# Attention into channel mix: whole-head value products in 64x64 tiles, natural channel order, and a new order of all tasks

## The chip, the cores and the metric

The kernel runs on one core of a Trainium2 chip. The metric is the device time of one execution in microseconds. Of the core's engines, PE multiplies matrices into PSUM, DVE, ACT and POOL work on vectors (POOL cannot read PSUM), and SP issues the DMAs. PEld is PE's loading of stationary operands.

## What is computed

Eight batches, eight heads, 576 positions, 64 channels a head. Causal attention in blocks of 64 positions feeds a channel mix over 512 channels:

```python
scores = scale * np.matmul(q, k.transpose(0, 1, 3, 2))
mask = block_i >= block_j                 # blocks of 64 positions
attn = np.exp(scores - max)               # masked
attn = attn / (np.sum(attn, axis=-1, keepdims=True) + 1e-09)
x = np.matmul(attn, v)                    # heads side by side: (B, S, 512)

xk = mu_k * x + (1.0 - mu_k) * x_prev     # x_prev: x one position earlier
xr = mu_r * x + (1.0 - mu_r) * x_prev
k = np.maximum(xk @ w_k, 0.0)             # 512 -> 1024
v = k * k @ w_v                           # 1024 -> 512
r = 1.0 / (1.0 + np.exp(-(xr @ w_r)))
out = r * v
```

## The kernel before, in words

The program is a list of some 930 tasks, each tied to an engine. Two tables drive it. ORDER is the sequence in which the tasks are issued, and so the order in which each engine's queue holds them; an entry `n+f` puts f filler products (128x512, of the identity matrix, read by nobody, L260) ahead of task n on PE. PLACE names the engine of each task that may run on several (A for ACT, D for DVE, P for POOL). Each engine works through its queue strictly in order; a task waits for its inputs and for its buffers. Buffers come in rings: "ld" (6 landing tiles for loads), "nl" (4 casts of q and k), "e" (exponentials, 16), "s" (3 PSUM tiles of two banks), "mm" (2 PSUM tiles of one bank), "xt", "d", "kr", "t", "o" and so on. A slot is free again when the last task that uses it has run.

Per batch b, the attention half goes as follows.

- Loads and turns: q and k are loaded and cast to bf16 (L247 on ACT, L251 on DVE and POOL), turned by PE against the identity (L354, into an "s" tile), and copied out (L247, L251) into "qkt". For batches 5 to 7 a DMA turns them instead. v is cast into "vo".
- Scores and exponentials: 12 units per batch. PE multiplies 64x64 tiles, four at a time (L413, an "s" tile); ACT takes the exponential of up to 1024 columns (L422) into an "e" tile.
- Sums, task "av S": with the constant `pick` PE sums the exponentials of each query over keys (L467, 128x32 tiles, 76 instructions), in three stretches of 192 positions; then it does the first 64 positions' products with the values. The rest of those products are tasks "av A" and "av B" (L478). A tile is 64x32: the 64 channels of a head are split into the even ones and the odd ones, f = 0 and 1, and A is f = 0 for all heads, B is f = 1. Each of S, A and B takes one "s" tile.
- Normalization on DVE: transpose the sums (t1, L507), take reciprocals (L512), transpose them back while they are spread over 32 rows (t2, L524), then three norms: T for the first 64 positions out of S (L536), A and B for the rest (L546), into "xt".
- Mix: the difference of neighbouring positions, one for each f (L568, POOL or DVE), and eight DVE pieces that write XK and XR (L585), one for each of four channel groups and of the two mixes.

The channel half works in nine chunks c of 512 positions: eight products with w_k ("pk", L632), relu (ACT L610 or DVE L612), squares (ACT L618, POOL or DVE L620), four products with w_r ("pr", L654) and a tanh (L663), four with w_v ("pv", L682), and the output on DVE (L690) and its store. A chunk's pk needs all four channel groups of XK for its positions, so chunk 0 starts when batch 0 is normalized and mixed, and chunk 1 needs batch 1. PE's queue interleaves the channel half of earlier positions with the attention half of later batches.

## Time and profile before

| what | value |
|---|---|
| median of 3 runs (range) | 264.22 us (263.5 to 264.7) |
| the profiled execution | 264.32 us, of which the span 262.5 us |
| busy in the span: PE, DVE, ACT, POOL | 246.8, 182.9, 180.4, 88.9 us |
| exponentials (L422) on ACT | 87.9 us |
| products with values (L478), instructions | 1280 |
| fillers (L260), instructions | 32 |

A busy time is the union of an engine's instructions. Matmuls are pipelined: several are in flight at once, so the mean time of one says little of their cost, which is read from how long a row of them takes. A row "a <-b" names in front what an instruction writes and behind what it reads; "[... <-X]" at its end is idle time of its engine and what ended it. The chain of waits is followed back from the last instruction: each row of it names a start, a length and the work that the end then hung on.

### The profile page before, as it was taken

How to read it: one execution, taken by the hardware profiler on the slowest of the kernel's cores; microseconds unless marked ns; L12 is line 12 of the kernel's file. 1: busy time of each engine (PE TensorE's matmuls, PEld its weight loads, DVE VectorE, ACT ScalarE, POOL GpSimd, SP SyncE). 2: the span in 40 equal slices, each digit the busy share in tenths (PEclk: the TensorE clock that was granted, in tenths of full speed). 3: DMA queues.
4: the chain of work that ended last, by engine and by line, in shares of the span. 5: the costliest groups of instructions: out<-in, count | busy, mean ns of one | idle time of the engine just before them, and what ended most of it. 6: DMA issues, size and time to landing. Idle time of an engine off the chain costs nothing.

```text
span 262.5 us, 7947 instructions
## 1 busy us (share of the span) xinstructions
PE 246.8 (94%) x3468; PEld 125.7 (48%) x3468; DVE 182.9 (70%) x245; ACT 180.4 (69%) x236; POOL 88.9 (34%) x71
## 2 busy tenths in 40 slices
PE   7687875999999999999999999999999999999995
PEld 2444643554545644544454446545544464444443
DVE  0153699589783897779889777496978497964423
ACT  1889897679888797857579897887457950460630
POOL 1115067169418600361531124802620246210130
PEclk9899999899999999999999999999999999999999
DMA  7999899799569993991999889976919200203105
GB/s 262 382 281 286 186 266 283 271 283 211 175 149 256 194 277 83 248 189 51 223 257 225 107 175 233 216 168 112 238 48 227 114 5 2 80 0 145 55 16 190
DMA packets 93428, 47.06 MB, mean 179 GB/s; under 512 B 81232, under 2 KB 81488, under 8 KB 93392
## 3 DMA queue, kind: packets, MB, share of 16 engines
q1 hardware_dynamic: 93392, 46.54, 73.0%
q8 instruction: 27, 0.44, 0.8%
q14 instruction: 9, 0.07, 0.1%
HBM read 33.56 MB, written 9.44 MB: 164 GB/s over the span
## 4 chain that ended last, share of the span: by engine, by line
PE 77%; DVE 7%; POOL 6%; ACT 5%; issue 2%; DMA 2%; SPq 0%; POOLq 0%; DVEq 0%
PE t_mm L632 23%; PE t_mm L682 21%; PE t_mm L654 11%; PE t_s L478 7%; PE t_s L413 7%; PE t_s L467 4%; ACT t_e L422 3%; PE t_s L354 3%; DVE XK L585 3%; DMA t_ld<-in_k_dram 2%; POOL t_k L620 2%; POOL t_d L568 2%; POOL t_nl L251 2%; ACT t_nl L247 1%; DVE t_o L690 1%
## 5 line engine op out<-in xcount | busy, mean ns | idle before, releaser
L422 ACT ACTIVATE t_e<-t_s 128x1024 f16<-128x1024 f32 (+1 forms) x96 | 87.9, 974 | 15.9 <-PE t_s L413 15.6
L632 PE MATMUL t_mm<-XK,WK 128*128 128x512 f16 x288 | 68.9, 383 | 1.8 <-POOL WK L251 1.2
L620 POOL TENSOR_TENSOR t_k<-t_kr 128x512 f16<-128x512 f32 x34 | 38.5, 1140 | 87.9 <-ACT t_kr L610 50.3
L682 PE MATMUL t_mm<-WV,t_k 128*128 128x512 f16 (+1 forms) x296 | 65.8, 374 | 0.3 <-POOL t_k L620 0.3
L610 ACT ACTIVATE t_kr<-t_mm 128x512 f32<-128x512 f32 x55 | 32.9, 598 | 27.3 <-PE t_mm L632 25.7
L632 PEld LDWEIGHTS <-WK 128*128 128x128 f16 x288 | 26.9, 98 | 36.1 <-issue 6.9
L682 PEld LDWEIGHTS <-t_k 128*128 128x128 f16 x296 | 28.0, 98 | 33.1 <-issue 1.9
L690 DVE SCALAR_TENSOR_TENSOR t_o<-t_t,t_mm 128x512 f32<-128x512 f32 (+1 forms) x37 | 24.6, 670 | 19.0 <-PE t_mm L682 13.7
L251 POOL CAST t_nl<-t_ld 128x1152 bf16<-128x1152 f32 x14 | 18.3, 1313 | 51.0 <-DVE XK L585 16.1
L663 ACT ACTIVATE t_t<-t_mm 128x512 f32<-128x512 f32 x36 | 21.5, 599 | 20.3 <-PE t_mm L654 20.0
L654 PE MATMUL t_mm<-WR,XR 128*128 128x512 f16 x144 | 34.9, 380 | 0.0
L585 DVE SCALAR_TENSOR_TENSOR XK<-t_d,MU,t_xt 128x576 f16<-128x576 f32 (+2 forms) x40 | 32.2, 834 | 1.5 <-POOL t_d L568 1.4
L413 PE MATMUL t_s<-t_qkt 64*64 64x64 bf16 (+7 forms) x640 | 29.2, 290 | 2.9 <-ACT t_e L422 1.8
L585 DVE SCALAR_TENSOR_TENSOR XR<-t_d,MU,t_xt 128x576 f16<-128x576 f32 (+2 forms) x40 | 29.5, 749 | 2.9 <-POOL t_d L568 2.9
L568 POOL TENSOR_TENSOR t_d<-t_xt 128x1152 f32<-128x1152 f32 x10 | 22.9, 2298 | 14.5 <-DVE t_xt L546 9.2
L413 PEld LDWEIGHTS <-t_qkt 64*64 64x64 bf16 x640 | 14.7, 106 | 20.2 <-issue 16.2
L478 PE MATMUL t_s<-t_e,t_vo 64*32 64x64 f16 (+7 forms) x1280 | 23.0, 284 | 0.0
L546 DVE TENSOR_TENSOR t_xt<-t_s,t_rt 128x1024 f32<-128x1024 f32 x16 | 19.4, 1220 | 5.0 <-PE t_s L478 4.6
L478 PEld LDWEIGHTS <-t_vo 64*32 64x32 f16 x1280 | 17.1, 92 | 7.2 <-issue 2.5
L654 PEld LDWEIGHTS <-XR 128*128 128x128 f16 x144 | 13.0, 98 | 15.4 <-issue 1.5
L354 PE MATMUL t_s<-identb,t_nl 128*128 128x128 bf16 x180 | 14.5, 237 | 5.5 <-ACT t_nl L247 2.4
L620 DVE TENSOR_TENSOR t_k<-t_kr 128x512 f16<-128x512 f32 x19 | 15.5, 832 | 6.1 <-ACT t_kr L610 5.8
(35 smaller groups left out, 177.9 us busy)
## 6 DMA issues: line engine op xcount, KB each, us to landing
t_ld<-in_v_dram SPq DMA_DIRECT2D x32, 288.0 KB, 5.9
out_dram<-t_o SPq DMA_DIRECT2D x35, 256.0 KB, 2.5
t_ld<-in_q_dram SPq DMA_DIRECT2D x10, 576.0 KB, 6.6
t_ld<-in_k_dram SPq DMA_DIRECT2D x10, 576.0 KB, 6.5
t_ld<-in_q_dram SPq DMA_DIRECT2D x12, 288.0 KB, 4.9
t_ld<-in_k_dram SPq DMA_DIRECT2D x12, 288.0 KB, 5.0
t_ld<-in_moe_w_k_dram SPq DMA_DIRECT2D x4, 512.0 KB, 6.9
t_ld<-in_moe_w_v_dram SPq DMA_DIRECT2D x4, 512.0 KB, 4.8
```

Source lines behind the costliest of these rows:

```text
L251: return e.tensor_copy(dst, src)
L413: nc.tensor.matmul(PS[g * D:g * D + D, x, col:col + n], qkt[rows, ka:ka + D], qkt[rows, qa:qa + n], start=True, stop=True)
L422: nc.scalar.activation(new(ebuf[key])[:, :, 0:width], new(m)[:, :, 0:width], AF.Exp, scale=ISQ)
L478: nc.tensor.matmul(dst(slice(c * QC, (c + 1) * QC), u, f, q0, n), weights(b, u, c, t, f), new(ebuf[key])[u * D:u * D + D, x, col:col + n], ...
L568: return e.tensor_tensor(new(d)[:, 0:2 * n].rearrange("p (u t) -> p u t", u=2), x[:, :, 1 + lo:1 + hi], x[:, :, lo:hi], ALU.subtract)
L585: return nc.vector.scalar_tensor_tensor((XK, XR)[kr][:, cc, g:g + w], new(d)[:, u * n + at - lo:u * n + at - lo + w], MU1[:, kr, cc:cc + 1 ...
L610: nc.scalar.activation(new(kr), new(m), AF.Relu)
L620: return e.tensor_tensor(dst(), KR, KR, ALU.mult)
L632: nc.tensor.matmul(ps, WK[:, cc, jc * P:(jc + 1) * P], XK[:, cc, at:at + CH], start=(cc == 0), stop=(cc == CCn - 1))
L654: nc.tensor.matmul(ps, XR[:, cc, g % R:g % R + P], WR[:, cc], start=(cc == 0), stop=(cc == CCn - 1))
L682: nc.tensor.matmul(ps[:, 0:w], k2[:, jc, jt * P:(jt + 1) * P], WV[:, jc, cols], start=(jc == 0), stop=(jc == JCn - 1))
L690: nc.vector.scalar_tensor_tensor(new(o)[:, 0:w], new(tb)[:, cols], 1.0, new(m)[:, 0:w], ALU.add, ALU.mult)
```

## The change

The products with values no longer split a head into even and odd channels. A tile is 64x64, a whole head; task A is now the even heads of each pair (x = 0), B the odd ones (x = 1), each for all rows of S and of its own tile. With that the channels stand in natural order, and the weights are loaded as two runs of 128 rows instead of 128 pairs of rows. The sums go in two stretches of 288 positions (60 instructions). Because two heads now lie on 64 rows each, the reciprocals are needed in two spreads, one for each x: after the reciprocal come a copy and four copies of 32 rows, then two transposes ("t2" for x = 0 and 1), each followed by a norm in two parts, first the tail out of S and then the rest. Both norms read S. mu_k and mu_r are loaded as rows and turned by one small product on PE. The ring "e" shrinks from 16 to 14, "rt" grows from 1 to 2. ORDER and PLACE are new throughout; there are 50 fillers.

```diff
-RINGS = {"ld": 6, "nl": 4, "qkt": 2, "vo": 2, "e": 16, "xt": 2, "tt": 1,
-         "rc": 2, "rt": 1, "d": 2, "kr": 5, "k2": 1, "t": 4, "o": 4,
+RINGS = {"ld": 6, "nl": 4, "qkt": 2, "vo": 2, "e": 14, "xt": 2, "tt": 1,
+         "rc": 2, "rt": 2, "d": 2, "kr": 5, "k2": 1, "t": 4, "o": 4,
 ORDER = """
-30 2 6 7 3 4+14 10 11 12 5 13 14 15 97 98 16 17 8 9 64+4 65 62 63 56 57
+3 4 5+14 6 7 8 11 12 13+9 14 15 9 10 16 17 18 45+5 46 53 49 50 47+2 48
...
-    QW = S // 3
+    NS = 2
+    QW = S // NS
...
     def mus(eng, me):
         for n, src in enumerate((moe_mu_k, moe_mu_r)):
-            nc.sync.dma_start(
-                MU[:, n].rearrange("p (g f) -> p g f", f=2),
-                src.rearrange("(g p f) -> p g f", g=2, f=2))
+            nc.sync.dma_start(MUR[CCn * n:CCn * n + CCn, :],
+                              src.rearrange("(c p) -> c p", p=P))
+    mu_rows = add("mus", "SP", mus)
+    mu_ps = plan.buf("mm")
+
+    def mut(eng, me):
+
+        nc.tensor.matmul(new(mu_ps)[:, 0:2 * CCn], MUR[:, :], identf,
+                         is_transpose=True, start=True, stop=True)
...
-                "(g p f) j -> g p f j", g=2, f=2)
+                "(g f p) j -> g p f j", g=2, f=2)
...
-        def products(some, dst, fs):
+        def products(some, dst, xs):
             end = max(t for _, (_, t, *_) in some)
-            for f in fs:
+            for x in xs:
                 for key, (y, t, col, q0, n) in some:
-                    for x in range(2):
-                        c = 2 * x + y
-                        for u in range(2):
-                            nc.tensor.matmul(
-                                dst(slice(c * QC, (c + 1) * QC), u, f, q0, n),
-                                weights(b, u, c, t, f),
-                                new(ebuf[key])[u * D:u * D + D, x,
-                                               col:col + n],
-                                start=t == 0, stop=t == end)
+                    for u in range(2):
+                        nc.tensor.matmul(
+                            dst(slice(y * D, (y + 1) * D), u, x, q0, n),
+                            new(vo_buf[b])[u * D:u * D + D, 2 * x + y, t],
+                            new(ebuf[key])[u * D:u * D + D, x, col:col + n],
+                            start=t == 0, stop=t == end)
...
         def rec(eng, me):
             J = W // cw
+            RC = new(rc)
             nc.vector.reciprocal(
-                new(rc)[:, :, 0:NB].rearrange("p u (j n) -> p u j n", j=J),
+                RC[:, 0].rearrange("p u (j n) -> p u j n", j=J),
...
+            nc.vector.tensor_copy(RC[:, 1], RC[:, 0])
+
+            for x in range(2):
+                for y in range(2):
+                    at, to = (2 * y + x) * QC, (2 * y + 1 - x) * QC
+                    nc.vector.tensor_copy(RC[to:to + QC, x],
+                                          RC[at:at + QC, x])
         t = add(f"rec {b} {part}", "DVE", rec, [t], [tt, rc])
...
+        for x in range(2):
+            def t2(eng, me, x=x):
+                nc.vector.transpose(
+                    new(rt[x])[:, 0:2 * W].rearrange("p (n r) -> p n r", r=QC),
+                    new(rc)[:, x].rearrange("p u n -> p (u n)").unsqueeze(
+                        2).to_broadcast([P, 2 * NB, QC]))
+            t2_ = add(f"t2 {b} {part} {x}", "DVE", t2, [t], [rc, rt[x]])
+
+            def norm(eng, me, x=x):
+                dst = new(xt_buf[b])[:, :, :].rearrange(
+                    "p (u x) t -> p x u t", x=2)[:, x]
+                nc.vector.tensor_tensor(
+                    dst[:, :, 1:1 + D],
+                    new(m["S"])[:, :, QW + x * D:QW + x * D + D],
+                    turned(x)[:, :, 0:D], ALU.mult)
+                nc.vector.tensor_tensor(
+                    dst[:, :, 1 + D:1 + S],
+                    new(m["AB"[x]])[:, :, 0:S - D],
+                    turned(x)[:, :, D:W], ALU.mult)
+            evac["x", b, part, x] = add(
+                f"norm {b} {part} {'AB'[x]}", "DVE", norm,
+                [av["S"], av["AB"[x]], t2_],
+                [m["S"], m["AB"[x]], rt[x], xt_buf[b]])
```

Three places of the new order matter below. The first is the head of SP's queue, before and then in the change; t_ld are the landing tiles.

```order
L268 DMA t_ld_58<-in_moe_w_r_dram 128x1024
L268 DMA t_ld_59<-in_q_dram 128x2x576
L268 DMA t_ld_60<-in_k_dram 128x2x576
L268 DMA t_ld_61<-in_q_dram 128x2x576
L268 DMA t_ld_62<-in_k_dram 128x2x576
```

```order
L271 DMA t_ld_58<-in_q_dram 128x2x576
L271 DMA t_ld_59<-in_k_dram 128x2x576
L271 DMA t_ld_60<-in_q_dram 128x2x576
L271 DMA t_ld_61<-in_k_dram 128x2x576
L271 DMA t_ld_62<-in_v_dram 64x18x64 x2
L283 DMA MUR<-in_moe_mu_k_dram 4x128
```

The load of w_r has left the head; batch 0's four loads of q and k come first, and mu follows the first load of v. The second place is DVE's queue from the sums of batch 0 (t_tt, t_rc, t_rt: sums, reciprocals and their transposes; t_s: the PSUM tiles; t_xt: normalized; t_d: differences) to the mix, before and then in the change.

```order
L507 STREAM_TRANSPOSE t_tt_108<-t_s_154 128x192
L512 RECIPROCAL t_rc_112<-t_tt_108 128x36
L524 STREAM_TRANSPOSE t_rt_117<-t_rc_112 128x1152
L536 TENSOR_TENSOR t_xt_103<-t_s_154,t_rt_117 128x4x64
L251 COPY t_qkt_74<-t_s_153 128x1152
L546 TENSOR_TENSOR t_xt_103<-t_s_152,t_rt_117 128x2x512
L285 TENSOR_SCALAR MU_175<-MU 128x8
L546 TENSOR_TENSOR t_xt_103<-t_s_153,t_rt_117 128x2x512
L568 TENSOR_TENSOR t_d_122<-t_xt_103 128x1152
L585 SCALAR_TENSOR_TENSOR XK<-t_d_122,MU_175,t_xt_103 128x576
```

```order
L513 STREAM_TRANSPOSE t_tt_106<-t_s_151 128x288
L519 RECIPROCAL t_rc_110<-t_tt_106 128x36
L523 COPY t_rc_110<-t_rc_110 128x36
L528 COPY t_rc_110<-t_rc_110 32x36 x4
L537 STREAM_TRANSPOSE t_rt_115<-t_rc_110 128x1152
L546 TENSOR_TENSOR t_xt_101<-t_s_151,t_rt_115 128x2x64
L550 TENSOR_TENSOR t_xt_101<-t_s_153,t_rt_115 128x2x512
L537 STREAM_TRANSPOSE t_rt_116<-t_rc_110 128x1152
L546 TENSOR_TENSOR t_xt_101<-t_s_151,t_rt_116 128x2x64
L550 TENSOR_TENSOR t_xt_101<-t_s_152,t_rt_116 128x2x512
L588 SCALAR_TENSOR_TENSOR XK<-t_d_120,MU_175,t_xt_101 128x576
L572 TENSOR_TENSOR t_d_121<-t_xt_101 128x1152
```

The copy of a turned q or k and mu's subtraction have left this place; the chain itself holds five copies, a second transpose and one norm more, and the first XK piece takes its difference from POOL. The third place is ACT's queue from the last exponential of batch 0 on (t_qkt: copies of turned q and k; t_nl and t_vo: casts; t_e: exponentials), before and then in the change.

```order
L422 ACTIVATE t_e_95<-t_s_154 128x1024
L247 COPY t_qkt_75<-t_s_153 128x1152
L247 COPY t_qkt_75<-t_s_152 128x1152
L422 ACTIVATE t_e_96<-t_s_153 128x1024
L422 ACTIVATE t_e_97<-t_s_152 128x1024
L422 ACTIVATE t_e_98<-t_s_154 128x1024
```

```order
L434 ACTIVATE t_e_95<-t_s_151 128x1024
L250 COPY t_qkt_75<-t_s_152 128x1152
L250 CAST t_nl_68<-t_ld_58 128x2x9x64
L250 COPY t_qkt_75<-t_s_153 128x1152
L250 COPY t_qkt_75<-t_s_152 128x1152
L250 CAST t_nl_67<-t_ld_59 128x2x9x64
L434 ACTIVATE t_e_96<-t_s_153 128x1024
L434 ACTIVATE t_e_97<-t_s_153 128x1024
L434 ACTIVATE t_e_84<-t_s_151 128x2x320
```

Where two copies stood between the batches' exponentials, three copies and two casts stand now, and the first two exponentials of batch 1 read the same PSUM tile.

More of the change, by code (lines that the diff above doesn't have):

```diff
@@ L219 @@
     make_identity(nc, identb)
-    pick = consts.tile([P, 3, QC], F16)
+    pick = consts.tile([P, NS, QC], F16)
     WK = consts.tile([P, CCn, DF], F16)
@@ L444, in add_av @@
         cw = QW
-        tt, rc, rt = plan.buf("tt"), plan.buf("rc"), plan.buf("rt")
+        tt, rc = plan.buf("tt"), plan.buf("rc")
+        rt = [plan.buf("rt") for _ in range(2)]
         late = [p for p in every if p[1][1:4:2] != (0, 0)]
@@ L522, in t2 @@
-        def t2(eng, me):
-            src = new(rc)[:, :, 0:NB]
-            nc.vector.transpose(
-                new(rt)[:, 0:2 * W].rearrange("p (n r) -> p n r", r=QC),
-                src.rearrange("p u n -> p (u n)").unsqueeze(
-                    2).to_broadcast([P, 2 * NB, QC]))
-        t2_ = add(f"t2 {b} {part}", "DVE", t2, [t], [rc, rt])
-        def norm(key, kind, fn):
-            evac["x", b, part, key] = add(
-                f"norm {b} {part} {key}", "DVE", fn, [av[kind], t2_],
-                [m[kind], rt, xt_buf[b]])
@@ L570, in diff @@
                     x[:, :, 1 + lo:1 + hi], x[:, :, lo:hi], ALU.subtract)
-            deps = [evac.get(("x", b, pt, key)) for pt in range(part + 1)
-                    for key in ("T", "AB"[f])]
+            deps = [evac["x", b, part, f]]
             sub = add(f"d {b} {part} {f}", ("POOL", "DVE"), diff, deps,
```

69 lines of the change are left out of this document (26 added, 43 removed), and 100 rows, old and new, of the table ORDER.

## The prediction

> **What bounds the kernel now.** I read the page first, then the table of stretches, the chain of waits, the groups by form, and the timeline of the first 50 us.
>
> ```profile
> span 262.5 us, 7947 instructions
> PE 246.8 (94%) x3468; PEld 125.7 (48%) x3468; DVE 182.9 (70%) x245; ACT 180.4 (69%) x236; POOL 88.9 (34%) x71
> 10.00:20.00 10.00, 8.45 (x102) 5.55 (x100) 4.81 (x5) 8.62 (x10) 2.18 (x2) 0.83 1.16 303
> 30.00:40.00 10.00, 7.98 (x213) 4.57 (x211) 9.22 (x9) 9.32 (x11) 5.04 (x3) 1.00 1.05 272
> 40.00:50.00 10.00, 7.65 (x137) 4.64 (x137) 8.96 (x9) 6.28 (x9) 5.51 (x4) 0.83 0.95 316
> 50.00:60.00 10.00, 10.00 (x203) 5.29 (x202) 6.74 (x10) 8.32 (x12) 5.28 (x5) 1.00 0.78 249
> 60.00:180.00 120.00, 119.18 (x1848) 60.16 (x1847) 94.52 (x129) 95.59 (x126) 44.62 (x34) 1.00 0.91 189
> 120.00:140.00 20.00, 19.65 (x308) 9.68 (x313) 17.99 (x24) 13.17 (x19) 6.37 (x5) 1.00 0.93 194
> ```
>
> Behind each stretch and its length stand the busy times of PE, weight load, DVE, ACT and POOL, then the granted clock, the DMA share and GB/s. There are two programs in one. From 50 us on PE never rests: a microsecond is gained there only by taking work from PE, and lost there only if another engine falls behind. Before 50 us PE waits for others, and two stretches show a clock of 0.83. There the length is set by a chain through ACT and DVE:
>
> ```profile
> 7.28 3.26 ACT L247 CAST t_nl<-t_ld 128x1152 bf16<-128x1152 f32 x3 [5.27 <-DMA t_ld<-in_k_dram]
> 10.26 0.76 DVE L251 CAST t_nl<-t_ld 128x1152 bf16<-128x1152 f32 x1 [8.97 <-DMA t_ld<-in_k_dram]
> 15.17 8.65 ACT L422 ACTIVATE t_e<-t_s 128x640 f16<-128x640 f32 x10 [0.44 <-PE t_s L413]
> 24.01 1.95 ACT t_e L422 x2
> 26.00 1.43 PE t_s L467 x76
> 28.62 1.39 DVE t_rt L524
> 36.17 4.74 DVE XK L585 x3
> 41.76 0.98 DVE XK L585
> 47.98 1.51 PE t_s L467 x64
> 73.62 1.02 PE t_mm L632 x4
> ```
>
> The first scores wait for loads, turns and copies; ACT then takes the twelve exponentials of batch 0 in 10.8 us (15.17 to 25.96); PE sums (26.00), DVE normalizes, mixes, and writes the fourth piece of XK at 42.74; the first product with w_k starts there. Batch 1 reaches its sums at 47.98 and its first product with w_k at 73.62.
>
> **The products: almost nothing.** PE's own price is read from stretches in which it streams without a wait.
>
> ```profile
> 226.17 7.13 PE t_mm L632 x32
> 89.68 1.32 PE t_s L478 x72
> 92.46 1.73 PE t_mm L682 x8
> 94.18 0.50 PE t_s L354 x9
> 94.69 0.56 PE t_s L413 x12
> 81.88 1.36 PE t_s L467 x76
> L478 PE MATMUL t_s<-t_e,t_vo 64*32 64x512 f16 x256 | 10.2, 380 | 0.0
> L413 PE MATMUL t_s<-t_qkt 64*64 64x512 bf16 x128 | 12.3, 388 | 0.8 <-ACT t_e L422 0.4 <-DVE t_xt L546 0.2
> ```
>
> A product of 512 columns takes 7.13/32 = 0.223 us when it stands alone. One A or B product runs through nine steps of 512, 512, 448, ... 64 columns, 2816 in all, with eight 64x32 tiles at a time: 2816/512 x 0.223 = 1.23 us, and the 72 instructions took 1.32. (256 instructions of 380 ns lie in 10.2 busy us: they overlap 9.5 deep.) So the time is that of the columns and not of the count. In the change four 64x64 tiles carry the same 2816 columns; that four run at once is what the scores show (128 x 388 ns in 12.3 us, 4.0 deep). The instructions halve, 1280 to 640, and the columns stay. The sums go from 76 to 60 instructions over the same 2880 columns, 1.25 of today's 1.36 us. Both sides: nothing, or all that lies above pure columns, 2 x 0.09 + 0.11 = 0.3 us a batch, 2.4 us in all. I take 0.4 us in all, near nothing, since the rest is mostly the change of the array's shape between kinds of product, of which the orders have about as many as before.
>
> The Trainium skill, TensorEngine Tiling (Array Packing), section Instruction Overhead, gives each matmul about 60 cycles of overhead on trn2. If those followed one another, an estimate from that page of 25 ns for each of 640 fewer products would be 16 us, and the time 248. The 72 instructions in 1.32 us, 18 ns each while streaming 1.23 us of columns, speak against it, and I keep it only as a rival.
>
> **What is added on DVE.** The durations of the pieces:
>
> ```profile
> 33.58 0.16 DVE L285 TENSOR_SCALAR MU<-MU 128x8 f32<-128x8 f32 x1
> L507 DVE STREAM_TRANSPOSE t_tt<-t_s 128x192 f32<-128x192 f32 x8 | 3.0, 379 | 12.3 <-PE t_s L478 12.3
> L512 DVE RECIPROCAL t_rc<-t_tt 128x36 f32<-128x36 f32 x8 | 3.0, 377 | 0.2
> L524 DVE STREAM_TRANSPOSE t_rt<-t_rc 128x1152 f32<-128x1152 f32 x8 | 11.0, 1375 | 0.2
> L536 DVE TENSOR_TENSOR t_xt<-t_s,t_rt 128x256 f32<-128x256 f32 x8 | 3.3, 418 | 0.1
> L546 DVE TENSOR_TENSOR t_xt<-t_s,t_rt 128x1024 f32<-128x1024 f32 x16 | 19.4, 1220 | 5.0 <-PE t_s L478 4.6
> L568 POOL TENSOR_TENSOR t_d<-t_xt 128x1152 f32<-128x1152 f32 x10 | 22.9, 2298 | 14.5 <-DVE t_xt L546 9.2 <-DVE t_xt L536 5.3
> L585 DVE SCALAR_TENSOR_TENSOR XK<-t_d,MU,t_xt 128x576 f16<-128x576 f32 x24 | 23.7, 1022 | 1.5 <-POOL t_d L568 1.4
> L251 DVE COPY t_qkt<-t_s 128x1152 bf16<-128x1152 bf16 x8 | 10.7, 1354 | 8.0 <-PE t_s L354 8.0
> L247 ACT COPY t_qkt<-t_s 128x1152 bf16<-128x1152 bf16 x12 | 13.3, 1121 | 1.9 <-PE t_s L354 1.7
> L252 DVE TENSOR_SCALAR WV<-t_ld 128x1024 f16<-128x1024 f32 x4 | 4.4, 1120 | 0.0
> L568 DVE TENSOR_TENSOR t_d<-t_xt 128x1152 f32<-128x1152 f32 x6 | 11.0, 1840 | 0.2
> L610 ACT ACTIVATE t_kr<-t_mm 128x512 f32<-128x512 f32 x55 | 32.9, 598 | 27.3 <-PE t_mm L632 25.7 <-POOL t_k L620 1.2
> L247 ACT CAST t_nl<-t_ld 128x1152 bf16<-128x1152 f32 x11 | 12.4, 1152 | 5.3 <-DMA t_ld<-in_k_dram 5.3
> ```
>
> Per batch: a second transpose of the reciprocals, 1.38 us; the first transpose 96 columns longer, 0.10 (1 ns a column, by 418 to 1220 ns for 768 more); the tail's norm in two halves, 2 x 0.29 instead of 0.42, so 0.16; and five copies of 36 columns, which no row shows: 0.16 us by the 128x8 row, 0.38 by the reciprocal of the same shape. I take 0.19 (the 128x8 row and 28 columns), so 0.95 us (0.8 to 1.9). Together 2.6 us a batch, 21 us in all, less some 6 us of casts and weight copies that the order moves to POOL: DVE goes from 183 to about 198 us, 75%. It has that room. What counts is the chain, since norm B now ends 0.48 + 1.33 + 1.38 + 1.51 + 1.38 + 1.51 = 7.6 us after the sums instead of 5.0, and the tile S, which two norms now read, comes free only then, not after 2.6 us. Of the three such tiles all are then taken, and the next scores, hence the exponentials, stand behind norm A.
>
> The mu change costs nothing: one product of 8 columns stands in PE's queue while ACT's exponentials keep PE waiting, and its two loads go out sixth, 20 us before use. Were that cover gone, it costs a load's wait of about 1.5 us once. The weights in natural order move as many bytes as before.
>
> **The front, walked through the new order** by these durations. (1) The first load, of w_r, leaves the head of the queue. Loads land 1.5 us apart (third at 7.28, fifth at 10.26), so the first lands at 4.3 and now q and k have 4.3, 5.8, 7.3, 8.8. The 14 fillers hold PE until 7.5; nine more stand behind the first turn (2.0 us at full clock). DVE's copy (1.35) and two casts (0.75 each) lead to the fourth turn at 11.0, ACT's two copies end at 12.8, the first exponential starts at 13.4 instead of 15.17. (2) Twelve take 10.8: 24.2. (3) Batch 0 is summed by 25.9, t1 ends 26.4, the reciprocals with copies 27.7, the transpose 29.1, norm A 30.6, norm B 33.5. (4) ACT does three copies and a cast, 4.5 us, before batch 1's first score may run, at 28.7; but it has no tile until norm A at 30.6. The first exponential of batch 1 starts at 31.0; the first two share one tile; the other ten (8.9, as 10.8 for twelve) with ACT's work between them, three copies (3.4), a cast (1.15) and three pieces of 0.6, run from 33.9 to about 49.2, against 47.98 before. That is 1.2 us lost. (5) In exchange POOL forms the difference 30.7 to 33.6, and one difference, one XR and four XK pieces put the first product with w_k at about 40.2 instead of 42.74. When batch 1's sums start at 49.2, seven of the eight w_k products of chunk 0 are done, not two, and one turn and one score more: 5 x 0.87 + 0.5 + 0.28 = 5.1 us of PE work (four instructions at 0.223 and a shape change for the first; a score is half of the 0.56). Less 1.2, the kernel is 3.9 us ahead.
>
> (6) Then DVE is late. From 50.8 its chain of 7.6 us, a wait of 0.7 for product A, two w_v casts (2.2), a difference (1.8) and eight pieces of 0.7 to 1.0 up to the last XK of batch 1 (7 us) bring chunk 1's first product to 70.0 instead of 73.62, with two turns less and one score more done (0.75). 2.9 us remain: about 1 us is given back in waiting for w_v and for XK.
>
> **The dense part.** PE's order after that has the same work. DVE gets 2.6 us a batch and loses 0.7: between 60 and 180, where five batches pass, it was busy 94.5 of 120 us and now comes to 104; ACT is as loaded as before. In batch 3 I find the XK of the next chunk some 16.2 us after the sums, and PE asking for it after 2 products with values (2.6), six w_k and w_r (5.2), four w_v (4 x 1.73) and eight scores (2.2), 16.9: a slack of 0.7 us. I put 0.5 us of stalls on the whole. Its end has the same last products and stores.
>
> Sum on the profiled execution, which took 264.3 (1.8 outside the span; the median of the runs is 264.2): 264.3 - 2.9 - 0.4 + 0.5 = 261.5.
>
> **Rivals.** *The chain from sums to XK decides each batch* (slower). Place: DVE between t1 and the last XK. It decides once the chain is more than 0.7 us a batch longer than I worked out: copies at 0.38 alone give 0.95 more, and POOL's difference at the slow end another. With both, the chain is 1.5 to 2 us longer; less the slack, six batches stall PE by about 0.8 us, 5 us, and step 6 loses another 1: 261.5 - 0.5 + 6 = 267, range 265.6 to 269. For it: DVE had 17.99 of 20 us in 120:140 and PE already lost 0.35 there. Against: over 60:180 it had 25 us of room.
>
> *The gain of the front goes back* (no change, 264). The first exponential comes no earlier, or a half-clock interval falls where the first w_k products stand. Today's clock of 0.83 in 10:20 and 40:50 is an interval of 3.4 us at half (0.17 x 10 / 0.5) after thin stretches. In the new order PE has only a score each microsecond, with a dozen fillers, from 31 to 40, so one may fall at 40; with three products in it that is 1 to 2 us. The Trainium skill, TensorE: Matmul & The Clock Gate, Part 1, says that one idle window of about 3.4 us halves the clock, in windows that do not start with the kernel; the 0.83 agrees.
>
> *The dense part costs nothing and step 6 does not stall* (259): the 3.9 us stay, with 1 us of shape changes saved.
>
> *The products do what their count says*: halved from 2.6 us to 1.3 a batch, 10.4 us less, 251. The streaming rows speak against it.
>
> **How the numbers follow.** Forecast 0.43 (260.0 to 262.9); front without give-back 0.18 (257 to 260); no change 0.20 (262.9 to 265.5); the chain 0.16; the products 0.03. What one can tell from no change is about 0.5%, 1.3 us. Faster 0.64, same 0.20, slower 0.16. The time is 261.5. The range leaves out the products, the upper half of the chain's cases and the outermost of the fast ones: 258.0 to 266.0.
>
> **What would show it.** Two products with values of a batch still take about 2.6 us of streaming PE. The first exponential starts near 13.4, batch 1's near 31, the first w_k product near 40, batch 1's sums near 49, chunk 1's first w_k product near 70; DVE's busy time is near 198 us; PE is solid after 72 us. It is wrong if PE shows gaps released by XK or t_k in each batch (the chain), if the clock row has a half interval between 34 and 45, if the first exponential comes after 14.5, or if a product pair falls to 1.3 us.

## The result and the profile after

The changed kernel takes 263.28 us (median of 15 runs, 261.38 to 265.75), the kernel before 264.7 beside it on the same chip (15 runs, 262.87 to 266.18). The ratio is 0.9939, 95% interval 0.9911 to 0.9967: faster by 0.6%, where 261.5 was forecast against 264.3, 1.1%. The profiled execution of the changed kernel took 263.92 us, of which the span 262.2.

First the head of the changed kernel's page and its table of stretches (columns as before: PE, weight load, DVE, ACT, POOL, then the clock, the DMA share and GB/s):

```profile
span 262.2 us, 6511 instructions
PE 247.7 (94%) x2719; PEld 123.8 (47%) x2719; DVE 195.0 (74%) x296; ACT 178.1 (68%) x237; POOL 92.3 (35%) x74
...
10.00:20.00 10.00, 7.99 (x95) 4.12 (x92) 2.95 (x4) 7.59 (x9) 2.02 (x2) 1.00 1.17 268
...
30.00:40.00 10.00, 7.90 (x116) 3.60 (x108) 9.89 (x12) 7.48 (x10) 5.05 (x3) 1.00 0.98 288
40.00:50.00 10.00, 9.28 (x85) 5.25 (x85) 8.97 (x12) 9.44 (x12) 5.25 (x5) 1.00 0.90 247
50.00:60.00 10.00, 9.99 (x178) 5.37 (x176) 9.04 (x15) 8.73 (x14) 6.24 (x6) 1.00 0.87 283
60.00:180.00 120.00, 117.50 (x1437) 58.75 (x1437) 103.77 (x160) 92.60 (x124) 41.28 (x31) 1.00 0.93 194
```

PE's instructions fell from 3468 to 2719 and its busy time did not fall. The clock is 1.00 in every stretch, where it was 0.83 in two. But between 60 and 180 us PE is busy 117.50 of 120 us, before 119.18: it now rests 2.5 us there instead of 0.8, and DVE has gone from 94.5 to 103.8. The chain of waits says the same by engine, before and after:

```profile
PE 77%; DVE 7%; POOL 6%; ACT 5%; issue 2%; DMA 2%; SPq 0%; POOLq 0%; DVEq 0%
```

```profile
PE 63%; DVE 22%; ACT 4%; DMA 3%; issue 3%; POOL 2%; SPq 1%; DVEq 0%; POOLq 0%
```

The marks of the walk, from the changed kernel's timeline and its chain of waits (start, length, what):

```profile
2.25 8.89 DMA t_ld<-in_k_dram
14.55 10.47 ACT L434 ACTIVATE t_e<-t_s 128x1024 f16<-128x1024 f32 x12 [1.92 <-PE t_s L425]
25.07 1.43 PE t_s L476 x57
32.47 1.02 ACT L434 ACTIVATE t_e<-t_s 128x1024 f16<-128x1024 f32 x1 [1.95 <-PE t_s L425]
41.24 1.89 PE L635 MATMUL t_mm<-XK,WK 128*128 128x512 f16 x8
50.69 1.36 PE t_s L476 x60
70.14 1.89 PE t_mm L635 x8
182.61 2.52 PE t_s L485 x72
```

(The exponentials now stand on L434, the sums on L476, the products with values on L485, w_k on L635.) Everything up to batch 1's sums is 0.6 to 1.5 us later than forecast; chunk 1's first product with w_k, at 70.14, is where it was forecast. Products A and B of a batch, 72 instructions, take 2.52 us (the last row); the 144 of before took 2.58, from the first of them to the next kind of work.

What was added on DVE, in the groups by form (busy us, mean ns):

```profile
L537 DVE STREAM_TRANSPOSE t_rt<-t_rc 128x1152 f32<-128x1152 f32 x16 | 21.7, 1368 | 0.2
L528 DVE COPY t_rc<-t_rc 32x36 f32<-32x36 f32 x32 | 5.6, 174 | 0.7
L546 DVE TENSOR_TENSOR t_xt<-t_s,t_rt 128x128 f32<-128x128 f32 x16 | 4.6, 291 | 0.5
L513 DVE STREAM_TRANSPOSE t_tt<-t_s 128x288 f32<-128x288 f32 x8 | 3.9, 483 | 7.5 <-PE t_s L485 7.5
L523 DVE COPY t_rc<-t_rc 128x36 f32<-128x36 f32 x8 | 3.4, 425 | 0.3
```

A batch pays 1.37 for the second transpose, 4 x 0.174 + 0.425 = 1.12 for the copies, 0.10 for the longer first transpose and 0.16 for the halved norm: 2.75 us. And this is where PE now rests, in its timeline (the bracket is the idle time before the row and what ended it):

```profile
92.14 1.02 PE L657 MATMUL t_mm<-WR,XR 128*128 128x512 f16 x4 [0.27 <-DVE t_o L693]
94.47 1.89 PE L685 MATMUL t_mm<-WV,t_k 128*128 128x512 f16 x8 [0.80 <-DVE t_o L693]
112.59 0.41 PE L425 MATMUL t_s<-t_qkt 64*64 64x512 bf16 x4 [0.58 <-DVE t_xt L550]
146.79 0.38 PE L685 MATMUL t_mm<-WV,t_k 128*128 128x512 f16 x1 [0.51 <-DVE t_o L693]
221.87 1.89 PE L685 MATMUL t_mm<-WV,t_k 128*128 128x512 f16 x8 [0.33 <-DVE t_o L693]
223.92 0.38 PE L635 MATMUL t_mm<-XK,WK 128*128 128x512 f16 x1 [0.17 <-DVE t_o L693]
```

These six make 2.66 us. Before, two rests after 72 us made 0.56:

```profile
73.62 0.59 PE L632 MATMUL t_mm<-XK,WK 128*128 128x512 f16 x2 [0.21 <-DVE t_o L690]
126.16 1.02 PE L632 MATMUL t_mm<-XK,WK 128*128 128x512 f16 x4 [0.35 <-DVE t_o L690]
```

None of the six waits for XK. Five wait for a t_mm tile that DVE has yet to empty into t_o (L693), one for a score tile that norm A (L550) has yet to free: work that stands in DVE's queue at the end of the chain or behind it.

So the account of the profiled pair closes to about 0.2 us: at 70.14 the kernel is 3.48 us earlier than before at the same product, with 0.75 us less work done (two turns less, one score more, the prediction's count), 2.7 ahead. It gives back 2.66 - 0.56 = 2.1 in rests. What is left, 0.6, stands beside 264.32 - 263.92 = 0.4 measured; the medians are 1.4 apart, and each kernel's runs scatter by 3.3 to 4.4 us. The rests in the rows are a lower bound of what PE loses, since part of a wait counts as busy there; the run without the longer chain, below, shows how much.

### The profile page after: what moved, and what is told of

The parts are those of the page before. It is cut to its first block, busy times and chain, and to the rows that moved or that the text cites. A ratio compares the mean times of both kernels' runs of the same rounds, so it can differ in the third digit from the quotient of the medians.

```text
span 262.2 us, 6511 instructions
## 1 busy us (share of the span) xinstructions
PE 247.7 (94%) x2719; PEld 123.8 (47%) x2719; DVE 195.0 (74%) x296; ACT 178.1 (68%) x237; POOL 92.3 (35%) x74
## 4 chain that ended last, share of the span: by engine, by line
PE 63%; DVE 22%; ACT 4%; DMA 3%; issue 3%; POOL 2%; SPq 1%; DVEq 0%; POOLq 0%
PE t_mm L635 23%; PE t_mm L685 16%; PE t_mm L657 8%; PE t_s L425 6%; DVE XK L588 4%; PE t_s L485 4%; PE t_s L476 4%; DVE t_xt L550 4%; ACT t_e L434 4%; DVE t_rt L537 3%; DMA t_ld<-in_k_dram 3%; PE t_s L366 2%; DVE t_o L693 2%; DVE XR L588 2%; DVE t_d L572 1%
## 5 line engine op out<-in xcount | busy, mean ns | idle before, releaser
L434 ACT ACTIVATE t_e<-t_s 128x1024 f16<-128x1024 f32 (+1 forms) x96 | 88.2, 984 | 24.5 <-PE t_s L425 24.2
L635 PE MATMUL t_mm<-XK,WK 128*128 128x512 f16 x288 | 68.2, 379 | 0.2 <-DVE t_o L693 0.2
L613 ACT ACTIVATE t_kr<-t_mm 128x512 f32<-128x512 f32 x54 | 32.1, 601 | 32.9 <-PE t_mm L635 32.6
L623 POOL TENSOR_TENSOR t_k<-t_kr 128x512 f16<-128x512 f32 x27 | 31.3, 1168 | 35.6 <-ACT t_kr L613 25.1
L635 PEld LDWEIGHTS <-WK 128*128 128x128 f16 x288 | 26.4, 97 | 32.4 <-issue 5.4
L693 DVE SCALAR_TENSOR_TENSOR t_o<-t_t,t_mm 128x512 f32<-128x512 f32 (+1 forms) x37 | 24.6, 670 | 18.3 <-PE t_mm L685 11.2
L425 PE MATMUL t_s<-t_qkt 64*64 64x512 bf16 (+7 forms) x640 | 30.7, 290 | 5.0 <-ACT t_e L434 3.1
L572 POOL TENSOR_TENSOR t_d<-t_xt 128x1152 f32<-128x1152 f32 x11 | 24.2, 2204 | 25.9 <-DVE t_xt L550 23.5
L588 DVE SCALAR_TENSOR_TENSOR XK<-t_d,MU,t_xt 128x576 f16<-128x576 f32 (+2 forms) x40 | 30.9, 802 | 1.9 <-POOL t_d L572 1.9
L588 DVE SCALAR_TENSOR_TENSOR XR<-t_d,MU,t_xt 128x576 f16<-128x576 f32 (+2 forms) x40 | 30.6, 782 | 0.2
L485 PE MATMUL t_s<-t_e,t_vo 64*64 64x64 f16 (+7 forms) x640 | 22.9, 285 | 0.3 <-ACT t_qkt L250 0.3
L537 DVE STREAM_TRANSPOSE t_rt<-t_rc 128x1152 f32<-128x1152 f32 x16 | 21.7, 1368 | 0.2
L623 DVE TENSOR_TENSOR t_k<-t_kr 128x512 f16<-128x512 f32 x22 | 17.0, 782 | 6.1 <-ACT t_kr L613 5.9
L485 PEld LDWEIGHTS <-t_vo 64*64 64x64 f16 x640 | 15.9, 107 | 8.6 <-issue 2.8
L550 DVE TENSOR_TENSOR t_xt<-t_s,t_rt 128x1024 f32<-128x1024 f32 x16 | 19.4, 1215 | 0.0
```

Source lines behind the costliest of these rows:

```text
L425: nc.tensor.matmul(PS[g * D:g * D + D, x, col:col + n], qkt[rows, ka:ka + D], qkt[rows, qa:qa + n], start=True, stop=True)
L434: nc.scalar.activation(new(ebuf[key])[:, :, 0:width], new(m)[:, :, 0:width], AF.Exp, scale=ISQ)
L485: nc.tensor.matmul(dst(slice(y * D, (y + 1) * D), u, x, q0, n), new(vo_buf[b])[u * D:u * D + D, 2 * x + y, t], new(ebuf[key])[u * D:u * D ...
L537: nc.vector.transpose(new(rt[x])[:, 0:2 * W].rearrange("p (n r) -> p n r", r=QC), new(rc)[:, x].rearrange("p u n -> p (u n)").unsqueeze(2) ...
L550: nc.vector.tensor_tensor(dst[:, :, 1 + D:1 + S], new(m["AB"[x]])[:, :, 0:S - D], turned(x)[:, :, D:W], ALU.mult)
L588: return nc.vector.scalar_tensor_tensor((XK, XR)[kr][:, cc, g:g + w], new(d)[:, u * n + at - lo:u * n + at - lo + w], MU1[:, kr, cc:cc + 1 ...
```

## Experiments

Two theories at the start. **A:** the products are worth nothing, the front gains near 3 us, and the longer chain on DVE takes most of it back later. **B:** the gain of the front was not there, or the products carry it.

**Each 64x64 product cut in two.**

```diff
-    for u in range(2):
-        nc.tensor.matmul(dst(slice(y * D, (y + 1) * D), u, x, q0, n),
-            new(vo_buf[b])[u * D:u * D + D, 2 * x + y, t], ...)
+    for h in range(2):
+        for u in range(2):
+            nc.tensor.matmul(dst(slice(y * D + h * QC, y * D + h * QC + QC), u, x, q0, n),
+                new(vo_buf[b])[u * D:u * D + D, 2 * x + y, t, h * QC:h * QC + QC], ...)
```

> The changed kernel, with each 64x64 product with values cut into two of 64x32 that stream the same columns (1280 instructions again, natural channel order kept). Theory of columns: PE's time for a batch's A and B stays at about 2.6 us, the whole at the changed kernel's time, within 0.3% (0.8 us); ratio to the kernel before 0.994 +- 0.004. Theory of counts: A and B take up to twice their time, +10 us, ratio about 1.03.

264.42 us, ratio to before 0.9998 (0.9968 to 1.0027), above the 0.994 +- 0.004 expected. A and B of a batch take 2.58 us again, 0.06 more than uncut, 0.5 us in all. In the profiled executions the sums of all eight batches start within 0.3 us of those of the changed kernel (batch 7 at 208.13 and 207.88), and the last matmul ends at 259.22 instead of 258.92. By the medians the cut costs more, 264.42 against 263.28, and the ratios, 0.9998 and the 0.9939 and 0.9957 of the uncut kernel's two measurements, say the same: about 1 us, so that by the times alone the products could carry most of the 1.4 us gained. The rows show 0.3 to 0.5 of it; the remainder is not settled. That 640 products more cost some 0.5 to 1 us, and not 16, is.

**No copies, no second transpose.** Both norms read the first spread, so half of the heads are divided by another head's sum; the chain is then about as long as before the change (some 5 us from the end of the sums), and everything else of the change stays.

```diff
-            nc.vector.tensor_copy(RC[:, 1], RC[:, 0])
-            ... (the four copies of 32x36)
+                if turns:
+                    return
+                turns.append(x)
                 nc.vector.transpose(
-                    new(rt[x])[:, 0:2 * W]...,
-                    new(rc)[:, x]...
+                    new(rt[0])[:, 0:2 * W]...,
+                    new(rc)[:, 0]...
```

> The changed kernel without the five copies and the second transpose of the reciprocals: both norms read the first spread, so the normalization of half the heads is left out of its right place; 2.6 us a batch leave DVE's chain. Theory that DVE's longer chain from sums to XK gives back the gain of the front: the waits of PE on DVE's output pieces near 92, 112, 146 and 222 us go, 1.5 to 2.5 us in the dense part, and batch 1's scores start 1.3 us earlier; 2.5 to 4 us in all, ratio 0.980 to 0.985. Rival, that PE's stalls come from POOL, ACT or the order itself and the chain has cover: not more than 0.5 us, ratio 0.992 or more.

258.39 us, ratio 0.9774 (0.9746 to 0.9801); 0.980 to 0.985 was expected. Its table of stretches:

```profile
60.00:180.00 120.00, 120.00 (x1498) 60.34 (x1497) 96.18 (x140) 94.67 (x126) 44.00 (x34) 1.00 0.92 191
```

PE does not rest at all between 60 and 180. This one run splits the change in two: all of it but the longer chain is worth 2.3%, some 6 us, and the longer chain gives some 5 of them back, in the medians 263.3 against 258.4. From the starts of the sums: batch 1 comes 1.7 us earlier than in the changed kernel (48.91 and 50.62), batch 2 2.8, batch 4 5.0, and from batch 5 on 5.7, of which 0.6 was there at batch 0, ahead of the first norm. Chunk 1's first product with w_k, in PE's timeline:

```profile
67.47 1.90 PE L632 MATMUL t_mm<-XK,WK 128*128 128x512 f16 x8
```

That is 2.7 us before the changed kernel's 70.14, 2.1 without the 0.6 of batch 0. From this product to the end of the last matmul this kernel takes 185.5 us (to 252.92) and the changed one, with the same products in the same order, 188.8 (to 258.92). So some 2 us of the chain's cost fall before this product, where the walk had counted the chain, and 3.3 behind it. The rests there differ by only 2.4 (2.66, and a single one of 0.25 here): a rest costs more than its row shows. The first rest of the changed kernel after 55 us, 0.24 at 60.4, is an example: from the scores ahead of it to the next products with w_v, at 61.21, it takes 1.13 us, and here, for the same 20 scores, 0.70.

**The copies twice**, meant as 1.2 us a batch more on the chain.

```diff
+            for _ in range(2):
                 nc.vector.tensor_copy(RC[:, 1], RC[:, 0])
...
+                    for _ in range(2):
                         nc.vector.tensor_copy(RC[to:to + QC, x], RC[at:at + QC, x])
```

> The changed kernel with each of the five copies made twice, the output the same: 1.2 us more per batch in the same chain. Theory of the chain: the front pays 1.2 to 2.5 us once or twice, and each tight batch 0.5 to 1 us more; 3 to 6 us in all, ratio 1.005 to 1.017. Rival (the chain has cover): under 1.3 us, ratio under 0.999.

270.12 us, ratio 1.0221 (1.0186 to 1.0256), 6.8 us over the changed kernel, where 1.005 to 1.017 was expected. By the groups by form the copies take 11.2 + 4.5 us in this kernel and 5.6 + 3.4 in the changed one: 6.7 us were added, 0.84 a batch and not 1.2, and practically all of them came out at the end. Of the 20 us that the run before took away (8 x 2.49), only 5 did. The changed kernel stands at the bend: a microsecond more on DVE's chain costs about one, one less gains about a quarter. The place that was short of a wait shows it, PE's timeline of this kernel:

```profile
115.87 0.41 PE L425 MATMUL t_s<-t_qkt 64*64 64x512 bf16 x4 [1.62 <-DVE t_xt L552]
```

It is the score that waited 0.58 us for norm A in the changed kernel; it now waits 1.62.

**Without the 36 fillers that follow the first 14.**

```diff
-3 4 5+14 6 7 8 11 12 13+9 14 15 9 10 16 17 18 45+5 46 53 49 50 47+2 48
+3 4 5+14 6 7 8 11 12 13 14 15 9 10 16 17 18 45 46 53 49 50 47 48
 ... (and so on, wherever +n stood behind a task)
```

> The changed kernel without the 36 fillers behind the first 14. Theory of the clock: an interval of 3.4 us at half clock or two come back between 10 and 50 us (granted clock under 1.00 there), and the first products with w_k come 0.5 to 1.5 us later; ratio 0.996 to 1.002. Rival, that fillers only fill waits: clock 1.00 and the time within 0.5 us of the changed kernel's, or earlier by up to 1 us since the nine fillers no longer stand in front of the second turn.

267.26 us, ratio 1.0115 (1.0066 to 1.0165), 4 us over the changed kernel; at most 2 were expected. Its table of stretches:

```profile
10.00:20.00 10.00, 5.45 (x78) 3.03 (x79) 2.87 (x3) 7.95 (x9) 2.29 (x2) 0.77 1.16 281
20.00:30.00 10.00, 8.86 (x129) 6.33 (x125) 2.92 (x7) 7.32 (x9) 4.38 (x4) 0.54 0.92 310
30.00:40.00 10.00, 6.76 (x132) 4.22 (x132) 9.84 (x12) 8.26 (x10) 4.21 (x2) 0.80 0.79 248
40.00:50.00 10.00, 8.67 (x69) 4.59 (x65) 7.22 (x9) 7.39 (x10) 5.17 (x4) 0.69 0.82 213
```

The clock falls to 0.77, 0.54, 0.80 and 0.69. Batch 1's sums come at 53.96 instead of 50.62, and all later ones keep these 3.4 us. So the full clock of the changed kernel is the fillers' doing, and part of the front's gain. The Trainium skill, TensorE: Matmul & The Clock Gate, Part 1, has the clock halved after one idle window of about 3.4 us. The shares missing here, 0.23, 0.46, 0.20 and 0.31 of 10 us each, are 24 us at half clock, about seven such windows, which agrees in kind; how little work makes a window idle no row shows, PE being busy 5.45 us of 10 in the thinnest stretch.

**The loads of v two places later.** The last load of q and k landed at 11.14 where 8.8 was forecast. In the changed kernel two loads of v are issued right behind it and share the transfer engines with it; here they stand behind three further loads of q and k:

```diff
-... 65 66 21 22 0 43+1 44 94 95 96 1 2 86 98 19 90 99 100 101 97 20 87 ...
+... 65 66 0 43+1 44 94 95 96 1 2 86 98 21 19 90 99 100 101 97 22 20 87 ...
```

> The changed kernel with batch 0's first load of v (and its cast) moved behind batch 1's first three loads of q and k, nothing else. Theory that the small rows of v, out fifth, slowed batch 0's last loads of q and k (they landed at 8.4 and 11.1 us where I had worked out 7.3 and 8.8): the fourth lands near 9, the first exponential starts near 13.4 instead of 14.55, and 0.5 to 1.2 us of it remain at the end; ratio 0.989 to 0.992. Rival, that loads take their turn whatever stands behind them: the fourth load again at about 11, ratio 0.994.

The ratio is 0.9962 (0.9934 to 0.9989), no different from the changed kernel's, where 0.989 to 0.992 was expected. ACT's timeline of this kernel:

```profile
13.30 10.46 ACT L434 ACTIVATE t_e<-t_s 128x1024 f16<-128x1024 f32 x12 [0.87 <-PE t_s L425]
```

With the four loads landed at 4.49, 5.94, 8.34 and 9.89 the first exponential starts 1.25 us earlier than in the changed kernel's profile, within 0.1 us of the forecast 13.4. That agreement is partly luck, since the third and fourth loads still land 1.0 and 1.1 us later than walked (7.3 and 8.8). Nor do the 1.25 us measure the edit: the start varies from one execution to the next. Ten profiled kernels of this document have v's loads in fifth place (all but the kernel before, this one and the combined one further below). Their fourth load lands between 9.31 and 11.34 and their first exponential starts between 12.72 and 14.75, the earliest in the kernel with the copies twice:

```profile
12.72 10.47 ACT L434 ACTIVATE t_e<-t_s 128x1024 f16<-128x1024 f32 x12 [1.06 <-PE t_s L425]
```

What holds in all ten is the distance from the third load to the fourth, 1.7 to 3.0 us; it is 1.5 here, in the combined kernel, which has the same order of loads, and in the kernel before. So v's loads do delay the last load of k. What that is worth at the end is not shown: each batch from the second on comes 0.9 us earlier here than in the changed kernel's profile (batch 3's sums at 104.93 and 105.83), but in the kernel with the differences moved, below, where v's loads stayed, they come at 105.04. The rests of PE later are the same (2.9 us after 55 in both).

**Three casts from DVE to ACT; two differences from POOL to DVE.** Two kernels, each with another relief for the stretch at 92 to 95.

```diff
 PLACE, one letter a task
-qk 4 0 0: D   qk 4 1 0: D   qk 4 0 1: D
+qk 4 0 0: A   qk 4 1 0: A   qk 4 0 1: A
```

> The changed kernel with three casts of batch 4's q and k moved from DVE to ACT, which stood in DVE's queue among the norms and XK pieces of batch 2 (2.3 us). Theory that PE waits there (0.27 and 0.80 us at 92 and 94 us) for DVE's output pieces behind that queue: the wait goes, 0.8 to 1.5 us, ratio 0.988 to 0.991. Rival, that the pieces wait for POOL's differences, not for the casts: less than 0.4 us, or a loss since ACT's relus come later; ratio 0.993 or more.

```diff
 PLACE, one letter a task
-d 2 0 0: P   d 7 0 1: P
+d 2 0 0: D   d 7 0 1: D
```

> The changed kernel with one of batch 2's two differences, and one of batch 7's, on DVE (1.35 us each) instead of POOL (2.3 each, in which DVE's XK pieces of 384 columns took 1.4 us each instead of 0.6). Theory that DVE and POOL slow each other there: batch 2's XK pieces end 0.5 to 1.5 us earlier, the first product with w_k of chunk 7 starts 0.5 us earlier and PE's gap at 221 to 224 goes; 0.5 to 1.5 us in all, ratio 0.988 to 0.992. Rival, that DVE's queue itself is full: DVE has 2.7 us more, the time is the same or up to 1 us longer, ratio 0.993 to 0.998.

Ratios 0.9971 (0.9938 to 1.0004) and 0.9968 (0.9937 to 0.9998): by the times alone neither is told from the changed kernel. In the traces the rests between 91 and 95, 1.07 us in the changed kernel, are 0.25 with the casts away and 0.64 with the differences away; in the second the rest at 221 grew from 0.33 to 0.63 in exchange (it stands at 219.0). So the casts on DVE and the differences on POOL beside it are both part of the cause there. All rests after 55 us together make 2.9 us in the changed kernel, 2.1 with the casts away and 2.6 with the differences away; in the times no gain shows, where 0.988 to 0.992 was expected of both.

**The reciprocal twice, and the cross copies of each spread right before its own transpose.** Meant to bring norm A forward, since the second spread's copies then stand behind it.

```diff
-            nc.vector.tensor_copy(RC[:, 1], RC[:, 0])
-            ... (the four copies of 32x36)
+            nc.vector.reciprocal(RC[:, 1]..., new(tt)[:, 0:cw]...)
...
             def t2(eng, me, x=x):
+                for y in range(2):
+                    nc.vector.tensor_copy(RC[to:to + QC, x], RC[at:at + QC, x])
                 nc.vector.transpose(...)
```

> The changed kernel with the reciprocal taken twice, straight into both spreads, and the two copies of each spread just ahead of its own transpose: the same output, the chain to the first norm about 0.55 us shorter and to the second about 0.2. Theory of the chain, by what the longer and the shorter chain did (6.8 us for 8 x 1.2 added, 4.9 for 8 x 2.6 taken away): 0.6 to 1.5 us faster than the changed kernel, ratio 0.988 to 0.992. Rival (only the second norm's end counts): 0.2 to 0.5 us, ratio 0.992 to 0.994.

It takes 278.61 us, ratio 1.0539 (1.0494 to 1.0583). That is some 17 us over the expectation. The groups by form and the timelines of DVE and POOL in that kernel:

```profile
L537 DVE COPY t_rc<-t_rc 32x36 f32<-32x36 f32 x32 | 22.0, 686 | 0.6
...
60.47 2.19 DVE L537 COPY t_rc<-t_rc 32x36 f32<-32x36 f32 x2
```

```profile
60.52 2.11 POOL L574 TENSOR_TENSOR t_d<-t_xt 128x1152 f32<-128x1152 f32 x1 [3.17 <-DVE t_xt L552]
```

The same copies, 174 ns each in the changed kernel, take 686 in the mean, 16.4 us more in all, which is about what the kernel lost (15 us). Two behind norm A take 2.19 us, just as long as the difference (L574) that norm A releases on POOL. Two explanations: this copy cannot run beside POOL's difference, or the place is late for any instruction.

**The same places, reciprocals instead of copies.**

```diff
-                    nc.vector.tensor_copy(RC[to:to + QC, x], RC[at:at + QC, x])
+                    nc.vector.reciprocal(RC[to:to + QC, x]..., new(tt)[at:at + QC, 0:cw]...)
```

> The same as the run with the reciprocal twice and each spread's two cross copies right before its own transpose, but the four copies of 32x36 are reciprocals of 32x36, read from the first transpose: the same places in DVE's queue, the same count, another operation, 0.32 us each instead of the copies' 0.17. Theory (it was the copies that waited for POOL's difference, and reciprocals do not wait for it): the 16 us are gone; the chain has 2.0 us between t1 and the last spread's transpose instead of 1.5 in the changed kernel, and at the slope of the run with the copies twice (6.8 us for 1.2 a batch) that is 2 to 3 us over the changed kernel, 265 to 267. Rival (any instruction at that place, behind norm A, waits, since it is the place that is late and not the kind of instruction): 276 to 280 as before.

267.63 us, ratio 1.0088 (1.0054 to 1.0122): 11 us of the 15 are gone with another operation in the same place. The same views of this kernel:

```profile
L537 DVE RECIPROCAL t_rc<-t_tt 32x36 f32<-32x36 f32 x32 | 11.8, 370 | 0.6
...
58.76 0.75 DVE L537 RECIPROCAL t_rc<-t_tt 32x36 f32<-32x36 f32 x2
```

```profile
58.80 2.11 POOL L579 TENSOR_TENSOR t_d<-t_xt 128x1152 f32<-128x1152 f32 x1 [3.05 <-DVE t_xt L557]
```

All 32 take 366 to 374 ns, beside the difference or not. It is the kind of instruction, its operation or what it reads (the reciprocals read the sums' tile and the copies their own), and not the place. The time is 0.6 us above the range expected, in part because they take 0.37 us each, where 0.32 was taken: the piece between the first transpose and the last spread's is 0.38 + 0.32 + 4 x 0.37 = 2.18 us, in the changed kernel 0.38 + 1.12 = 1.50. That is 0.68 a batch more, 5.4 us in all; at the slope of the doubled copies, about one for one, all of it would come out, and 4.2 did.

**Put together**: the loads, the casts and the differences of the three runs above, and a second reciprocal in place of the copy of 128x36 (0.32 us for 0.43).

```diff
-            nc.vector.tensor_copy(RC[:, 1], RC[:, 0])
+            nc.vector.reciprocal(RC[:, 1]..., new(tt)[:, 0:cw]...)
 (and the edits of the order and of PLACE shown above)
```

> The three edits that each took something off the changed kernel, in one kernel: the loads of v behind the last two of q and k, three casts of q and k from DVE to ACT, two differences from POOL to DVE. Beside them, a second reciprocal of the same shape (0.32 us by the earlier trace, not slowed beside POOL) takes the place of the copy of all 36 columns (0.43 us mean). Theory (the start is set by the last load of q and k; later DVE's chain stalls PE for some 3 us in all, in a few places): the start's 0.9 us and about half of the stalls go, so 261 to 262.3, some 1.5 us under the changed kernel on the same chip, ratio to the kernel before 0.987 to 0.992. Rival (the three edits gave one and the same microsecond, each moving a stall elsewhere): 262.8 to 263.5, no better than the best of the three alone.

> The changed kernel as it is, on the same chip as the combination, for the comparison. Both theories: 263.0 to 263.8, ratio 0.993 to 0.997.

Together 261.29 us (260.96 to 262.22), ratio 0.9865 (0.983 to 0.9901); the changed kernel on the same chip 263.46 (262.23 to 265.25), ratio 0.9957 (0.9928 to 0.9987). Together the edits are worth 2.2 us between the medians, where single ones could not be told from nothing. Its table of stretches:

```profile
60.00:180.00 120.00, 118.73 (x1430) 58.97 (x1432) 101.36 (x164) 96.36 (x128) 39.51 (x30) 1.00 0.91 191
```

PE rests 1.3 us there, between the changed kernel's 2.5 and none. This version is faster than both kernels. The second reciprocal has no part in that by the rows: with it and the four copies, which take 202 ns each here, DVE is busy 2.6 + 6.5 us, and 3.4 + 5.6 in the changed kernel. How the 2.2 us divide over the other three edits is not shown. That the time is the one forecast for the change is a coincidence.

## Why the prediction was right and where it was off

The direction was right, the size was half: forecast 2.8 us, measured 1.4 in the medians. The time lies inside the range, but above the likeliest case's own and in the one that the prediction had kept for no change (262.9 to 265.5).

- **Products: almost nothing.** Right. 72 instructions take 2.52 us, where 144 took 2.58; cutting them again costs 0.5 us in PE's rows. The rival of 251 is out, and so is the sum that hung on the overhead per instruction.
- **Added on DVE, 2.6 us a batch.** Right: 2.75. DVE came to 195 us in all (198), and to 103.8 between 60 and 180, forecast 104. The copies are 1.12 instead of 0.95, since 128x36 takes 0.425 in the mean and not 0.19: 0.18 us at 78.80, where POOL does nothing, and 0.57 at 27.74 and 0.93 at 53.29, beside work on POOL.
- **Step 1, first exponential 13.4.** Off by 1.15. The walk took the distances of the loads from the old kernel, where only loads of large rows lay in flight; v's loads, issued fifth, were not walked; they put the fourth load 1.7 to 3.0 us behind the third instead of 1.5. With them moved away the first exponential starts at 13.30. In the ten profiles with v's loads in place it starts between 12.72 and 14.75, so part of the 1.15 is scatter, and no gain at the end is shown.
- **Steps 2 to 5.** The lengths hold, so every mark carries the late start: sums 25.07 (25.9 was the end forecast; the sums here ran beside the last exponential), batch 1's first exponential 32.47 (31.0), w_k 41.24 (40.2), batch 1's sums 50.69 (49.2).
- **Step 6.** 70.14 for 70.0, by two errors that cancel: 1.4 us late on the way in, and then rests of 0.24 and 0.07 us at 60.4 and 70.1 where about 1 was put down.
- **The dense part, 0.5 us of stalls.** This is the step that failed. Its rests measured 2.1 us more than before, and the cost of the chain there, by the run without it, is 3.3. The slack was worked out for one request only, PE's for XK, and there it holds: no rest after 72 is ended by XK. But the chain of 2.75 us stands in DVE's queue ahead of other things too: t_o, which frees the tiles of products with w_v and w_r, and norm A, which frees the score tile. Their slack was not worked out, and they are what PE waits for. The busy shares, which the prediction held against the rival (25 us of room), said nothing of it: the changed kernel still has 16 us of room between 60 and 180 (120 - 103.8), and the doubled copies took 6.8 us.
- **The rivals.** *The chain decides each batch*: half true. It is the right mechanism and the wrong release; its 6 us of stalls come some 0.8 us a batch later than the change stands, where the doubled copies are. *Half-clock interval*: not here; the clock is 1.00 throughout, and the run without fillers shows what several of them cost, 4 us. *Dense part costs nothing*, 259: the run without the longer chain, at 258.4, shows such a dense part, but that rival had kept the chain.

## What to carry to other kernels

When work is added to a chain on an engine that is not the bound, work out the slack of everything queued behind it there, not only of the chain's own end: each tile that this engine frees for the bound is a due time. Busy shares do not tell how near the bend is; doubling the added work, and taking it away, does. And before a load is moved ahead, walk the loads that then lie in flight beside it, with the bytes per row that they move.

## What the hardware showed that was not expected

**Copies on DVE wait for POOL.** A copy of 32x36 takes 174 ns alone; right behind norm A two of them took 2.19 us beside a difference of 2.11 on POOL, while a reciprocal of the same shape takes 370 at either place. The copy of 128x36 shows it in the changed kernel itself: 0.18 us at 78.80, where POOL does nothing, and 0.93 at 53.29, ending 0.05 us behind POOL's instruction (DVE's timeline, then POOL's):

```profile
53.29 0.93 DVE L523 COPY t_rc<-t_rc 128x36 f32<-128x36 f32 x1
```

```profile
53.13 1.04 POOL L623 TENSOR_TENSOR t_k<-t_kr 128x512 f16<-128x512 f32 x1
```

The Trainium skill, SBUF — State Buffer, section SBUF: two separate sides, says that DVE and GpSimd share a port pair that one of them holds for a whole instruction, taken on DVE's side by operations in a 2-port mode or, against a GpSimd operation that reads SBUF, with two SBUF inputs. The trace agrees with the lock, the copy being held up until POOL's instruction ends and the reciprocal not; which mode each of them runs in no row shows. The second kind, two inputs, shows in the changed kernel at 87, where XK reads a difference and the normalized values while POOL forms the next differences (chain of waits, then POOL's timeline):

```profile
87.37 2.07 DVE XK L588
```

```profile
84.64 4.69 POOL L572 TENSOR_TENSOR t_d<-t_xt 128x1152 f32<-128x1152 f32 x2 [1.80 <-DVE t_xt L550]
```

The piece of 128x384 ends at 89.44, 0.1 us behind POOL, and took 2.07 us; those at 92.02 and 93.21, without POOL, take 0.60 and 0.61. The run with the differences moved to DVE bears it out: there POOL's only difference of this batch ends at 86.55, and the first two pieces, at 88.35 and 88.88, take 0.60 us each. That it is the port for which the piece waits is the skill's account; the rows show the wait for POOL.

**Loads of short rows slow the long ones beside them.** All transfers between 10 and 12 us, in the kernel before and in the changed one:

```profile
DMA packets 349, 0.77 MB, mean 384 GB/s; under 512 B 16, under 2 KB 16, under 8 KB 349
```

```profile
DMA packets 1303, 0.33 MB, mean 164 GB/s; under 512 B 1299, under 2 KB 1303, under 8 KB 1303
```

Nearly four times the packets, less than half the bytes. The ten profiles with v's loads in fifth place show 124 to 249 GB/s in these two microseconds, the two with v later 393 and 404; v's rows are of 256 B, and the other loads beside q and k there have long rows. The last load of k landed 1.7 to 3.0 us behind the load ahead of it in the ten, and 1.5 in the two. The queue that issues is held up too, SP's timeline of the changed kernel:

```profile
2.76 3.37 SPq L271 DMA_DIRECT2D t_ld<-in_v_dram  x2
6.17 4.49 SPq L283 DMA_DIRECT2D MUR<-in_moe_mu_k_dram  x1
```

The load of mu_k, 2 KB, takes 4.49 us of SP's time behind v's two (2.27 to 4.62 in the ten profiles), and batch 1's first loads of q go out at 11.01. With v's loads later it takes 0.41, and they go out at 3.53. The prediction had put the loads of mu down at nothing; their place was harmless, what stood ahead of them was not.
